# One pair of d_ff chunks by seven block products in tiles 3 to 6, and the visits of scores moved together

## The chip, the cores and the metric

The kernel runs on one core of one Trainium2 chip. The time is the device time of one execution in microseconds. The kernel before took 352.29 us (median of 3 runs, 351.99 to 355.41).

## What is computed

Block-wise causal attention over 8 batches, 8 heads, 576 positions and a head size of 64, and behind it a gated feed-forward network over all 4608 tokens:

```python
scores = scale * np.matmul(q, k.transpose(0, 1, 3, 2))      # q, k, v: 8 x 8 x 576 x 64
scores = np.where(block_i >= block_j, scores, -1e9)         # blocks of 64 positions
attn = np.exp(scores - max); attn = attn / (sum + 1e-09)
x = np.matmul(attn, v)                                      # as 4608 x 512
...
gate = np.maximum(x @ w_gate, 0.0)                          # 512 x 1536
val = x @ w_val                                             # 512 x 1536
return (gate * val @ w_out).astype(np.float32)              # 1536 x 512
```

## The kernel before, in words

The work falls into tiles of 512 tokens, j = 0 to 7 (one for the first 512 positions of each batch), and a ninth one that gathers the last 64 positions of every batch. A tile needs `xT`, the transposed output of its batch's attention. While tile j runs through the feed-forward network, the attention of batch j + 1 is made beside it.

**A tile's two halves.** In the first half d_ff is taken in 12 chunks `f` of 128. For each, four matmuls of 512 columns (the four blocks of d_model) give a gate, which ScalarE (ACT) puts through relu into `gate_sb`, and four give a value; VectorE (DVE) multiplies both into `hT` (`product` L936, `relu` L945, `hidden` L952). Gates and values lie in the three banks `ffnp` of PSUM; each is free again when its relu or its product on DVE has read it. In the second half `hT` times `wo` gives the output. From tile 2 on (`SEVEN`) this is done by seven block products instead of eight (`seven_products` L797), in matmuls of 256 columns; their left sides are sums and differences of chunks of `hT`, made on DVE by `Sums.make_part` (L762). A chunk of `wo` pairs is called c, 0 to 5.

**Pairs.** In tiles 7 and 8 the first half as well takes three pairs of chunks (2 and 3, 4 and 5, 6 and 7; `PAIRS`) by seven block products: `by_pairs` (L963) and in it `pair` (L1019). Their left sides are sums of weights, made once (`up_sum` L713, DVE); their right sides are sums of blocks of x (`x_sums` L905, DVE, into `perm`). The products of a pair accumulate in three places, y, z and m1, which ACT copies and DVE adds in between. In `pair` they are three tiles of their own (`bank` L388, L1023 to L1028).

**A visit of scores.** For each pair of heads (a round r, four a batch) PE writes the scores into two double banks `sc`, into `one` and into an `ffnp` bank; ACT takes their exps in four instructions (two of 512 columns, two of 1024; `visit` L431). The step `s` of a round issues the scores and the first three exps, `e` the fourth exp, `c` zeroes the masked corners on DVE, `a` and `b` multiply by v for the two heads (`head_av` L615, into `one` and `ffnp`) and normalise on DVE, and `x` issues the transposing DMA into `xT` on SP's queue. `L` is the score of the last keys.

**The order.** All engines but the DMAs follow the order in which the program issues (`manual_schedule`). The feed-forward network is a generator that yields after each matmul of 512 columns or two of 256; every other step has a place, a number of yields (`AT` L1325), and runs when the generator has come that far (L1748). A tile has 144 places; `place_of` (L1741) turns places into yields, since tiles from 2 on have 138. In tiles 3 to 6 a round's steps lie 28 places apart, with offsets from `STEADY` (L1608); the loads of q, k (`l`, place 9) and v (`lv`, 46) go on POOL's queue behind a product of `hidden`, and the transposing loads of q and k (`d`, place 66) on SP's. A wait between engines is a semaphore that the layer below the kernel sets from what instructions read and write.

What sets the end of a wait at the change are these lines: the banks of `pair` and the offsets of a round.

```python
y, z, m1 = bank("sc"), bank("one"), bank("sc")                      # pair, L1028
...
STEADY = {"s": 2, "e": 8, "c": 15, "a": 22, "b": 26, "x": 26.1}     # L1608
...
here = ("sc", "sc") if i == 3 else ("one", "ffn")                   # L1707
...
AT[f"{n}{r}"] = base + 28 * i + p                                   # L1710
```

Of the kernel before, what the change touches and what calls it, by code (L numbers as in the profile page):

```python
# [10 lines left out]
FP = mybir.dt.float32  # L11
# [6 lines left out]
def kernel(  # L18
# [20 lines left out]
    FIRST = 3  # L39
    SEVEN = 2  # L40
    PAIRS = (2, 4, 6)
    BASE = {0: 0, 1: 512, 3: 896, 2: 1024}
    AW = 1600
    TW = 256
# [63 lines left out]
    def new_bf():  # L108
        return [sb.tile([128, 2048], BF, name=n, bufs=2) for n in ("q_bf", "k_bf")]
# [603 lines left out]
    def up_sum(n, which):  # L713

        if not ups:
            ups["free"] = [
                t[:, 512 * i : 512 * i + 512].rearrange("p (c f) -> p c f", c=2)  # L720
                for two in (new_bf(), new_bf())
                for t in two
                for i in range(4)
            ]
        i, lo = divmod(PAIRS[n], 4)
        f = slice(128 * lo, 128 * lo + 256)
        g, u = wg[i], wv[i]
        a, b, op = {
            1: (g[:, 0:2, f], u[:, 2:4, f], AX.add),
            2: (u[:, 0:2, f], u[:, 2:4, f], AX.add),  # L730
            5: (g[:, 0:2, f], g[:, 2:4, f], AX.add),
            6: (u[:, 0:2, f], g[:, 0:2, f], AX.subtract),
            7: (g[:, 2:4, f], u[:, 2:4, f], AX.subtract),
        }[which]
        t = ups[n, which] = ups["free"].pop(0)
        nc.vector.tensor_tensor(out=t, in0=a, in1=b, op=op)

    class Sums:
# [58 lines left out]
    def seven_products(j, quads, sums):  # L797

        def times(to, which, p, c, first):
            two = wo[c // 2][:, 2 * (c % 2) : 2 * (c % 2) + 2, :]
            t = sevens[c // 2][:, 768 * (c % 2) : 768 * (c % 2) + 768]
            right = {  # L810
                5: two[:, 1, 256:512],
                2: two[:, 0, 0:256],
                1: t[:, 0:256],
                3: two[:, 0, 256:512],
                4: two[:, 1, 0:256],
                6: t[:, 256:512],
                7: t[:, 512:768],
            }[which]
            nc.tensor.matmul(  # L819
                to,  # L820
                sums.of(c)[which][:, 128 * p : 128 * p + 128],
                right,
                start=first,
                stop=(c == 5),
                skip_group_check=True,
            )

        def half(to, p):
            return to[:, 256 * p : 256 * p + 256]

        early, last = ((0, 1, 2, 3), (4, 5)) if j < B - 1 else ((0, 1, 2, 4), (3, 5))

        def whole(to, which, new=True, cs=range(6)):
            for p in range(2):
                for c in cs:
                    times(half(to, p), which, p, c, new and (p, c) == (0, 0))
                    if c % 2:
                        yield

        def store_later(hi, n0, ob, p0=0, p1=2):  # L840
            if store:
                store.pop()()
            if j < B:
                store.append(lambda: put_block(j, hi, n0, ob, p0, p1))
            else:
                put_block(j, hi, n0, ob, p0, p1)

        y = psum_ffn.tile([128, 512], FP, name="ffnp")
        z = psum_one.tile([128, 512], FP, name="one")
        for to, which in ((y, 5), (z, 2)):  # L850
            yield from whole(to, which, cs=early)
        for to, which in ((y, 5), (z, 2)):
            yield from whole(to, which, new=False, cs=last)
        for q in range(3) if j >= B - 1 else ():
            sums.make_part(q, 1, 0, 2)
        g = sb.tile([128, 512], FP, name="ob", bufs=5)
        nc.scalar.copy(g, y)
        nc.vector.tensor_tensor(out=g, in0=z, in1=g, op=AX.add)
        for q in range(3) if j >= B - 1 else ():
# [12 lines left out]
        yield from whole(z, 4, new=False)  # L872
        c21 = sb.tile([128, 512], FP, name="ob", bufs=5)
        nc.scalar.copy(c21, z)
        store_later(1, 0, c21)
        nc.gpsimd.tensor_tensor(out=g, in0=g, in1=c21, op=AX.add)
        m6 = psum_ffn.tile([128, 512], FP, name="ffnp")
        yield from whole(m6, 6)
        nc.vector.tensor_tensor(out=c22, in0=m6, in1=c22, op=AX.add)
        store_later(1, 256, c22)  # L880
        if j < B:
            m7 = psum_ffn.tile([128, 512], FP, name="ffnp")
            yield from whole(m7, 7)
            nc.vector.tensor_tensor(out=g, in0=g, in1=m7, op=AX.subtract)
            store_later(0, 0, g)
        else:
            for p in range(2):
                m7 = psum_ffn.tile([128, 512], FP, name="ffnp")[:, 0:256]
                for c in range(6):
                    times(m7, 7, p, c, c == 0)  # L890
                    if c % 2:
                        yield
                nc.vector.tensor_tensor(
                    out=half(g, p), in0=half(g, p), in1=m7, op=AX.subtract
                )
                store_later(0, 0, half(g, p), p, p + 1)
# [34 lines left out]
    def ffn_gen():  # L931
        for j in range(B + 1):
# [30 lines left out]
            def by_pairs():  # L963
# [15 lines left out]
                def value(f):  # L979
                    to = psum_ffn.tile([128, 512], FP, name="ffnp")  # L980
                    for c in range(4):
                        product(to, 1, c, f)
                        yield
                    nc.vector.tensor_tensor(
                        out=quads[f // 4][:, f % 4], in0=gates[f], in1=to, op=AX.mult
                    )

                def times(to, n, which, new):
# [30 lines left out]
                def pair(n, first, second, third=()):  # L1019
# [37 lines left out]
                        op1=AX.mult,  # L1057
                    )

                while len(sums.two) < 3:  # L1060
                    sums.two.append(sb.tile([128, 2048], BF, name="stage", bufs=10))
                yield from gate(0)
                store.pop()()
                if j < B:
# [20 lines left out]
                yield from value(11)  # L1085
                sums.make_part(2, 0, 1, 2)

            if j >= B - 1:
                yield from by_pairs()
                yield from seven_products(j, quads, sums)  # L1090
                continue
# [141 lines left out]
    with tc.manual_schedule(engines={E.PE, E.DVE, E.Activation, E.Pool, E.SP}):  # L1233
# [371 lines left out]
            "cv00/23": "pool",  # L1605
            "cv01": "pool",
        }
        STEADY = {"s": 2, "e": 8, "c": 15, "a": 22, "b": 26, "x": 26.1}  # L1608
        acts = {
            "Lq0": lambda: e0.load_qk(0, 2, nc.scalar),  # L1610
            **{f"Lq{h}": lambda h=h: e0.load_qk(h, 2) for h in (2, 4, 6)},
# [91 lines left out]
        for b in range(4, B):  # L1703
            base = 144 * (b - 1)
            for i in range(4):
                r = 4 * b + i
                here = ("sc", "sc") if i == 3 else ("one", "ffn")  # L1707
                acts.update(round_at(r, ("dve", *here, None)))
                for n, p in STEADY.items():
                    AT[f"{n}{r}"] = base + 28 * i + p  # L1710
                    if i == 3 and n in "abx":
                        AT[f"{n}{r}"] += 5
                    if n == "s":
                        AT[f"{n}{r}"] += (0, 1, 2, 1)[i]
            acts[f"L{b}"] = lambda b=b: last_keys(b)
            AT[f"L{b}"] = base + 11
# [10 lines left out]
        acts["X"] = lambda: x_sums(B, (4,))  # L1727
        AT["X"] = 1003
        for i in range(15):
            n, which = i // 5, (5, 2, 1, 6, 7)[i % 5]  # L1730
            acts[f"U{i}"] = lambda n=n, which=which: up_sum(n, which)
            AT[f"U{i}"] = (
                820 + 5 * i if i < 8 else 878 + 28 * (i - 8) if i < 10 else 964 + 8 * (i - 10)
            )
        for c in range(6):
            AT[f"W{c}"] = (225, 229, 233, 242, 266, 270)[c]
# [4 lines left out]
        def place_of(p):  # L1741

            j, o = divmod(p, 144)
            if j < SEVEN:
                return p
            return 144 * SEVEN + 138 * (j - SEVEN) + min(o, 96) + max(0, o - 96) * 42 / 48

        for n in sorted(acts, key=lambda n: AT[n]):  # L1748
            at = int(place_of(AT[n]))
# [33 lines left out]
```

## Time and profile before

| | |
|---|---|
| median of 3 runs | 352.29 us (351.99 to 355.41) |
| the profiled execution's own time | 352.26 us |
| its span, first to last instruction | 350.5 us |
| mean granted TensorE clock | 0.995 |
| tile 4, from its first gate to tile 5's | 213.98 to 251.13 us |
| of it the first half, the second half | 24.32 us, 12.83 us |

PE is TensorE's matmuls, PEld its weight loads, ACT is ScalarE, DVE VectorE, POOL GpSimd, SP the sync engine, which here only issues DMAs. A matmul's row lasts from its start until its result is out; the next one starts much earlier, so the distance of two starts is what a matmul costs on PE. On ACT and DVE too a row's end can overlap the next row's start by about 0.1 us. A row's bracket tells the idle time before it and the instruction that ended it.

### The profile page before, as it was taken

Reading aid. Unit: us, or ns where it says so; the run is one execution under the profiler, and the core shown is the slowest. Engines: PE = TensorE matmul, PEld = TensorE weight load, DVE = VectorE, ACT = ScalarE, POOL = GpSimd, SP = SyncE. Lnnn points to the kernel's source line nnn. Section 1 sums busy time; section 2 is a strip of 40 time slices with the busy share of each in tenths; the row PEclk is TensorE's granted clock in tenths of the full one; section 3 lists DMA queues with packets and bytes.
Section 4 is the critical chain, followed back from the end, with each engine's and each line's share of the span. In section 5 each row is a group of like instructions: output and inputs, shape, how many; then the busy total and the mean of one; then the engine's idle time right before and its main releaser. Section 6 shows DMA issues by size and latency. Waiting matters only on the chain.

```text
span 350.5 us, 8301 instructions
## 1 busy us (share of the span) xinstructions
PE 342.1 (98%) x3245; PEld 208.0 (59%) x3245; DVE 223.9 (64%) x557; ACT 186.0 (53%) x298; POOL 154.9 (44%) x196
## 2 busy tenths in 40 slices
PE   6899999999999999999999999999999999999994
PEld 3554455545545568555855576556755687687673
DVE  4654445768518784467547772668567867986892
ACT  4942757587335862666355546555366525423521
POOL 4857556488966802590149203950300022213213
PEclk9899999999999999999999999999999999999999
DMA  8999989999999996899359944999310031003005
GB/s 245 294 352 373 348 222 280 191 153 177 173 222 107 145 183 129 103 147 165 65 134 138 141 101 124 128 141 143 115 47 15 18 93 51 2 0 123 1 2 120
DMA packets 155399, 50.02 MB, mean 143 GB/s; under 512 B 134464, under 2 KB 151744, under 8 KB 155360
## 3 DMA queue, kind: packets, MB, share of 16 engines
q0 software_dynamic: 70528, 8.98, 48.6%
q1 hardware_dynamic: 76432, 31.47, 43.1%
q10 hardware_dynamic: 8400, 9.05, 8.1%
q8 instruction: 25, 0.41, 0.5%
q14 instruction: 14, 0.11, 0.1%
HBM read 37.75 MB, written 9.44 MB: 135 GB/s over the span
## 4 chain that ended last, share of the span: by engine, by line
PE 94%; DVE 2%; ACT 1%; POOL 1%; issue 0%; POOLq 0%
PE ffnp L937 46%; PE ffnp L819 12%; PE ffnp L1168 6%; PE one L819 5%; PE sc L1003 3%; PE sc L454 3%; PE one L454 2%; PE one L589 2%; PE ffnp L589 2%; PE one L1003 2%; PE one L937 2%; ACT attnT L418 1%; PE sc L589 1%; PE one L1219 1%; PE ffnp L551 1%; PE ffnp L273 1%
## 5 line engine op out<-in xcount | busy, mean ns | idle before, releaser
L947 ACT ACTIVATE gate_sb<-ffnp 128x512 bf16<-128x512 f32 x95 | 57.1, 605 | 74.9 <-PE ffnp L937 70.9
L937 PE MATMUL ffnp<-xT,wg 128*128 128x512 bf16 x356 | 96.7, 379 | 0.0
L937 PE MATMUL ffnp<-xT,wv 128*128 128x512 bf16 x328 | 90.9, 380 | 0.0
L957 DVE TENSOR_TENSOR hT<-gate_sb,ffnp 128x512 bf16<-128x512 bf16 x76 | 52.0, 684 | 45.3 <-PE ffnp L937 28.6
L937 PEld LDWEIGHTS <-wv 128*128 128x128 bf16 x384 | 35.4, 98 | 37.2 <-issue 4.2
L459 ACT ACTIVATE attnT<-sc 128x1024 bf16<-128x1024 f32 x56 | 57.0, 1042 | 0.0
L937 PEld LDWEIGHTS <-wg 128*128 128x128 bf16 x384 | 35.7, 98 | 34.8 <-issue 1.4
L871 POOL TENSOR_TENSOR ob<-ob 128x512 f32<-128x512 f32 x7 | 9.6, 1371 | 102.3 <-ACT ob L868 53.9
L819 PEld LDWEIGHTS <-stage 128*128 128x128 bf16 x420 | 40.3, 98 | 6.0
L778 DVE TENSOR_TENSOR stage<-hT 128x512 bf16<-128x512 bf16 (+2 forms) x82 | 37.8, 493 | 0.9
L589 PEld LDWEIGHTS <-attnT 128*128 128x128 bf16 x640 | 26.7, 98 | 11.7 <-DVE attnT L1228 1.1
L819 PE MATMUL ffnp<-stage 128*128 128x256 bf16 x252 | 31.4, 273 | 0.0
L342 POOL DMA_DIRECT2D q_bf<-in_q_dram x20 | 18.0, 909 | 20.5 <-DVE hT L957 9.7
L466 ACT ACTIVATE attnT<-one 128x512 bf16<-128x512 f32 (+1 forms) x28 | 15.0, 535 | 21.0 <-PE ffnp L454 14.7
L342 POOL DMA_DIRECT2D v_bf<-in_v_dram x30 | 24.2, 878 | 2.4 <-DMA q_bf<-in_q_dram 1.3
L1168 PE MATMUL ffnp<-wo,hT 128*128 128x512 bf16 x96 | 23.6, 379 | 0.0
L454 PEld LDWEIGHTS <-kTm 64*128 64x128 bf16 x384 | 11.0, 94 | 15.1 <-issue 7.9
L342 POOL DMA_DIRECT2D k_bf<-in_k_dram x20 | 18.1, 945 | 0.0
L1034 POOL TENSOR_TENSOR ob<-ob 128x512 f32<-128x512 f32 x6 | 7.7, 1275 | 23.2 <-ACT ob L1033 23.2
L819 PEld LDWEIGHTS <-hT 128*128 128x128 bf16 x168 | 16.4, 98 | 1.9
L454 PE MATMUL sc<-qTm,kTm 64*128 64x512 bf16 (+1 forms) x168 | 16.8, 305 | 0.0
L868 ACT COPY ob<-ffnp 128x512 f32<-128x512 f32 x7 | 4.1, 585 | 22.1 <-PE ffnp L819 22.1
(192 smaller groups left out, 557.1 us busy)
## 6 DMA issues: line engine op xcount, KB each, us to landing
out_dram<-ob ACTq DMA_DIRECT2D x32, 256.0 KB, 2.4
stage<-in_moe_w_val_dram SPq DMA_DIRECT2D x6, 512.0 KB, 8.6
stage<-in_moe_w_gate_dram SPq DMA_DIRECT2D x6, 512.0 KB, 8.6
stage<-in_moe_w_out_dram SPq DMA_DIRECT2D x6, 512.0 KB, 10.6
q_bf<-in_q_dram POOLq DMA_DIRECT2D x20, 128.0 KB, 4.3
k_bf<-in_k_dram POOLq DMA_DIRECT2D x20, 128.0 KB, 5.3
v_bf<-in_v_dram POOLq DMA_DIRECT2D x20, 128.0 KB, 6.2
stage<-in_v_dram SPq DMA_DIRECT2D x19, 128.0 KB, 5.4
```

The lines of the kernel that those rows point to most:

```text
L342: ins = nc.gpsimd.dma_start(dst, part_of)
L454: nc.tensor.matmul(o, kTm[b % 2][head_of(hh), c, hp, :], qT, start=True, stop=True)
L459: return lambda: nc.scalar.activation(at[:, :, lo : lo + 512], sc, AF.Exp, scale=scale)
L466: nc.scalar.activation(at[:, hh, 1024 : 1024 + w], third[hh][:, 0:w], AF.Exp, scale=scale)
L589: nc.tensor.matmul(av[:, p, :], at[:, col : col + 128], v_bf[b % 2][:, c, h, :], start=(p == 0), stop=(c == p), skip_group_check=True,)
L778: nc.vector.tensor_tensor(out=out.rearrange("p (c n) -> p c n", c=m), in0=a, in1=b, op=op)
L819: nc.tensor.matmul(to, sums.of(c)[which][:, 128 * p : 128 * p + 128], right, start=first, stop=(c == 5), skip_group_check=True,)
L937: nc.tensor.matmul(to, (wg, wv)[t][f // 4][:, c, 128 * (f % 4) : 128 * (f % 4) + 128], x[:, c], start=(c == 0), stop=(c == 3),)
L947: nc.scalar.activation(gate_sb, gate, AF.Relu)
L957: nc.vector.tensor_tensor(out=h, in0=gate_sb, in1=val, op=AX.mult)
L1003: nc.tensor.matmul(to[:, 256 * k : 256 * k + 256], left[:, c, 128 * k : 128 * k + 128], right[:, c], start=new and (k, c) == (0, 0), stop= ...
L1168: nc.tensor.matmul(op, hT[f][:, 128 * s : 128 * (s + 1)], wo[f // 4][:, f % 4, n0:n1], start=(f == 0), stop=(f == 11),)
```

## The change

Tiles 3 to 6 (and no longer only 7 and 8) run `by_pairs`, but in a shape of their own. Chunks 0 to 3, 8, 9, 4, 5, 10 and 11 are taken as gate and value, in this order; chunks 6 and 7 are one pair, run by the new function `middle`, behind gate 5. It differs from `pair` in its places: y and z are the two halves of one double bank, m1 is in the other; and z is added to y's copy by DVE, where `pair` copies z too and lets POOL add.

```diff
+                def middle(n, halves):
...
+                    yz = psum_sc.tile([128, 2, 512], FP, name="sc")
+                    y, z = yz[:, 0, :], yz[:, 1, :]
+                    m1 = bank("sc")
+                    low, a, b = ob(), ob(), ob()
+                    yield from times(y, n, 5, True)
+                    nc.scalar.copy(a, y)
+                    yield from times(z, n, 2, True)
+                    nc.vector.tensor_tensor(out=a, in0=z, in1=a, op=AX.add)
+                    yield from halves[0]
+                    yield from times(m1, n, 1, True)
+                    nc.vector.tensor_tensor(out=a, in0=m1, in1=a, op=AX.subtract)
+                    yield from times(y, n, 3, False)
+                    high = relu(y)
+                    yield from times(z, n, 4, False)
+                    nc.scalar.copy(low, z)
+                    yield from halves[1]
+                    yield from times(y, n, 6, False)
+                    nc.vector.tensor_tensor(out=b, in0=y, in1=a, op=AX.add)
+                    yield from times(z, n, 7, False)
+                    nc.vector.tensor_tensor(out=a, in0=z, in1=a, op=AX.add)
+                    nc.vector.tensor_tensor(
+                        out=h[:, :, 256:512], in0=split(high), in1=split(b), op=AX.mult
+                    )
+                    nc.vector.scalar_tensor_tensor(
+                        out=h[:, :, 0:256],
...
+                if j < B - 1:
+                    yield from both(0)
+                    x_sums(j, (1,))
+                    yield from gate(1)
+                    store.pop()()
+                    yield from value(1)
+                    x_sums(j, (3,))
+                    yield from both(2)
+                    x_sums(j, (4, 6))
+                    yield from both(3)
+                    x_sums(j, (7,))
+                    yield from both(8)
+                    sums.make_part(0, 0, 0, 2)
+                    yield from both(9)
+                    sums.make_part(0, 1, 0, 2)
+                    yield from both(4)
+                    sums.make_part(0, 2, 0, 2)
+                    sums.make_part(2, 0, 0, 1)
+                    yield from gate(5)
+                    yield from middle(MIDDLE, (value(5), gate(10)))
+                    yield from value(10)
+                    sums.make_part(1, 0, 0, 2)
+                    yield from gate(11)
+                    yield from value(11)
+                    sums.make_part(2, 0, 1, 2)
+                    return
...
-            if j >= B - 1:
+            if j > SEVEN:
                 yield from by_pairs()
```

In the second half the order of c changes, and parts 1 and 2 of the sums for chunks 4 to 11 are made inside it:

```diff
-        early, last = ((0, 1, 2, 3), (4, 5)) if j < B - 1 else ((0, 1, 2, 4), (3, 5))
+        early, last = ((0, 1, 2, 3), (4, 5)) if j == SEVEN else ((0, 1, 2, 4), (3, 5))
+
+        late_parts = range(3) if j >= B - 1 else (1, 2) if j > SEVEN else ()
```

The four visits of batches 4 to 7 get places of their own, 16 apart and from 5 places before the tile's start, so that the last one's product with v lies in the tile's first half; its banks are `one` and `ffnp` like the others'. The last keys (`L`) go from place 11 to 4. The five weight sums of the pair that tiles 3 to 6 use are made in tile 2's second half, in two buffers `stage` that are kept; those of the other two pairs stay where they were.

```diff
-        STEADY = {"s": 2, "e": 8, "c": 15, "a": 22, "b": 26, "x": 26.1}
+        STEADY = (
+            (-5, 4, 10, 16, 19.5, 19.6),
+            (12, 20, 26, 34, 37.5, 37.6),
+            (28, 36, 42, 50, 53.5, 53.6),
+            (44, 52, 58, 66, 69.5, 69.6),
+        )
...
-                here = ("sc", "sc") if i == 3 else ("one", "ffn")
+                here = ("one", "ffn")
...
-            n, which = i // 5, (5, 2, 1, 6, 7)[i % 5]
+            n, which = (2, 0, 1)[i // 5], (5, 2, 1, 6, 7)[i % 5]
...
-                820 + 5 * i if i < 8 else 878 + 28 * (i - 8) if i < 10 else 964 + 8 * (i - 10)
+                390 + 8 * i if i < 5 else 820 + 8 * (i - 5) if i < 10 else 964 + 8 * (i - 10)
```

More of the change, by code (lines that the diff above doesn't have):

```diff
@@ L41 @@
     PAIRS = (2, 4, 6)
+    MIDDLE = 2
     BASE = {0: 0, 1: 512, 3: 896, 2: 1024}
@@ L713, in up_sum @@
     def up_sum(n, which):
-        if not ups:
-            ups["free"] = [
+        kept = n == MIDDLE
+        if kept not in ups:
+            ups[kept] = [
                 t[:, 512 * i : 512 * i + 512].rearrange("p (c f) -> p c f", c=2)
-                for two in (new_bf(), new_bf())
-                for t in two
+                for t in (
+                    [sb.tile([128, 2048], BF, name="stage", bufs=10) for _ in range(2)]
+                    if kept
+                    else [*new_bf(), *new_bf()]
+                )
                 for i in range(4)
@@ L734, in up_sum @@
         }[which]
-        t = ups[n, which] = ups["free"].pop(0)
+        t = ups[n, which] = ups[kept].pop(0)
         nc.vector.tensor_tensor(out=t, in0=a, in1=b, op=op)
@@ L853, in seven_products @@
             yield from whole(to, which, new=False, cs=last)
-        for q in range(3) if j >= B - 1 else ():
+        for q in late_parts:
             sums.make_part(q, 1, 0, 2)
@@ L858, in seven_products @@
         nc.vector.tensor_tensor(out=g, in0=z, in1=g, op=AX.add)
-        for q in range(3) if j >= B - 1 else ():
+        for q in late_parts:
             sums.make_part(q, 2, 0, 2)
@@ L983, in value @@
                         yield
-                    nc.vector.tensor_tensor(
-                        out=quads[f // 4][:, f % 4], in0=gates[f], in1=to, op=AX.mult
+                    products.append(
+                        nc.vector.tensor_tensor(
+                            out=quads[f // 4][:, f % 4], in0=gates[f], in1=to, op=AX.mult
+                        )
                     )
@@ L1058, in pair @@
                     )
+                def middle(n, halves):
+                    q, k0 = divmod(PAIRS[n], 4)
+                    h = quads[q][:, k0 : k0 + 2]
+                    yz = psum_sc.tile([128, 2, 512], FP, name="sc")
[18 more added lines that the diff above has]
+                    nc.vector.tensor_tensor(out=a, in0=z, in1=a, op=AX.add)
+                    nc.vector.tensor_tensor(
+                        out=h[:, :, 256:512], in0=split(high), in1=split(b), op=AX.mult
+                    )
+                    nc.vector.scalar_tensor_tensor(
+                        out=h[:, :, 0:256],
+                        in0=split(a),
+                        scalar=0.0,
+                        in1=split(low),
+                        op0=AX.max,
+                        op1=AX.mult,
+                    )
@@ L1060, in by_pairs, with both @@
+                def both(f):
+                    yield from gate(f)
+                    yield from value(f)
                 while len(sums.two) < 3:
                     sums.two.append(sb.tile([128, 2048], BF, name="stage", bufs=10))
+                if j < B - 1:
[24 more added lines that the diff above has]
+                    return
@@ L1607 @@
         }
-        STEADY = {"s": 2, "e": 8, "c": 15, "a": 22, "b": 26, "x": 26.1}
+        STEADY = (
[3 more added lines that the diff above has]
+            (44, 52, 58, 66, 69.5, 69.6),
+        )
         acts = {
@@ L1706 @@
                 r = 4 * b + i
-                here = ("sc", "sc") if i == 3 else ("one", "ffn")
+                here = ("one", "ffn")
                 acts.update(round_at(r, ("dve", *here, None)))
[L1709 to L1714, printed above, removed]
+                for n, p in zip("secabx", STEADY[i]):
+                    AT[f"{n}{r}"] = base + p
             acts[f"L{b}"] = lambda b=b: last_keys(b)
-            AT[f"L{b}"] = base + 11
+            AT[f"L{b}"] = base + 4
             if b + 1 < B:
@@ L1745, in place_of @@
                 return p
-            return 144 * SEVEN + 138 * (j - SEVEN) + min(o, 96) + max(0, o - 96) * 42 / 48
+            paired = max(0, j - SEVEN - 1)
+            up = 96 if j == SEVEN else 94
+            return (
+                144 * SEVEN + 138 * (j - SEVEN) - 2 * paired
+                + min(o, up) + max(0, o - 96) * 42 / 48
+            )
         for n in sorted(acts, key=lambda n: AT[n]):
```

## The prediction

> **What bounds the kernel now.** I read the page's list of engines first, then busy time by window for one tile of the steady part (tile 4, 213.98 to 251.13 us), then the timeline around a visit of scores and around a pair by block products, which today only tiles 7 and 8 have.
>
> ```profile
> PE 342.1 (98%) x3245; PEld 208.0 (59%) x3245; DVE 223.9 (64%) x557; ACT 186.0 (53%) x298; POOL 154.9 (44%) x196
> ```
> ```profile
> 213.98:238.30 24.32, 24.32 (x231) 12.28 (x228) 15.42 (x41) 14.93 (x24) 13.76 (x17) 1.00 1.60 129
> 238.30:251.13 12.83, 12.83 (x141) 10.47 (x140) 9.89 (x28) 5.24 (x9) 2.89 (x2) 1.00 0.73 125
> ```
> The window lines give length, then busy time of PE, PEld, DVE, ACT and POOL. In both halves of the tile PE is busy for every microsecond at clock 1.00; the list of PE's waits for 177 to 288 us is empty. So a matmul saved in tiles 3 to 6 is time saved, and any wait put in front of PE is time lost. One visit (222.68 is its first score, 223.44 the matmul behind it):
>
> ```profile
> 222.68 0.28 PE L454 MATMUL one<-qTm,kTm 64*128 64x256 bf16 x1
> ...
> 223.11 0.60 ACT L466 ACTIVATE attnT<-one 128x512 bf16<-128x512 f32 x1 [0.38 <-PE ffnp L454]
> ...
> 223.44 0.39 PE L937 MATMUL ffnp<-xT,wv 128*128 128x512 bf16 x1
> ...
> 223.60 0.59 ACT L466 ACTIVATE attnT<-ffnp 128x512 bf16<-128x512 f32 x1
> 223.67 1.03 PE L937 MATMUL ffnp<-xT,wg 128*128 128x512 bf16 x4
> ...
> 224.08 1.03 ACT L459 ACTIVATE attnT<-sc 128x1024 bf16<-128x1024 f32 x1
> ...
> 224.53 1.03 PE L937 MATMUL ffnp<-xT,wv 128*128 128x512 bf16 x4
> ...
> 224.98 0.62 ACT L947 ACTIVATE gate_sb<-ffnp 128x512 bf16<-128x512 f32 x1
> ...
> 225.66 0.69 DVE L957 TENSOR_TENSOR hT<-gate_sb,ffnp 128x512 bf16<-128x512 bf16 x1 [0.31 <-ACT gate_sb L947]
> ```
> Read from it: four matmuls of 512 columns take 0.86 (223.67 to 224.53), 0.216 each; a relu that stands behind a visit's first three exps starts 2.30 after the first score and ends at 2.92, and its product on DVE ends at 3.67. Now the pair of tile 7:
>
> ```profile
> 291.36 0.60 PE L1003 MATMUL sc<-perm,wg 128*128 128x256 bf16 x4
> 291.79 0.60 PE L1003 MATMUL sc<-perm,wv 128*128 128x256 bf16 x4
> ...
> 291.99 0.60 ACT L947 ACTIVATE gate_sb<-sc 128x512 bf16<-128x512 f32 x1 [1.05 <-PE sc L1003]
> ...
> 293.09 0.60 PE L1003 MATMUL sc<-perm,q_bf 128*128 128x256 bf16 x4
> ...
> 293.53 0.60 PE L1003 MATMUL sc<-perm,k_bf 128*128 128x256 bf16 x4
> 293.79 0.69 DVE L1044 TENSOR_TENSOR ob<-sc,ob 128x512 f32<-128x512 f32 x1 [0.27 <-PE sc L1003]
> ```
> Four matmuls of 256 columns issue in 0.436 (0.109 each) and end 0.60 after the first's start. The product into z (291.79) starts before ACT has read y (291.99), since y and z are two tiles there. ACT follows the last end (291.96) by 0.03, DVE (293.69) by 0.10. And the one place where PE waits for a full bank:
>
> ```profile
> 274.03 0.69 DVE L957 TENSOR_TENSOR hT<-gate_sb,ffnp 128x512 bf16<-128x512 bf16 x1
> ...
> 274.77 0.59 PE L937 MATMUL ffnp<-xT,wv 128*128 128x512 bf16 x2
> ```
> DVE ends at 274.72 and PE goes on 0.05 later: the price of a hand-over to PE.
>
> **The change, part by part.** All in us, for one of tiles 3 to 6.
>
> Columns: chunks 6 and 7 lose 16 matmuls of 0.216 (3.46) and get 28 of 0.109 (3.05): 0.40 less.
>
> Inside the pair: `middle` takes y and z as the two halves of one tile `yz`. In the list of built instructions with their semaphores, z's first matmul of product 2 waits for ACT's copy of y, that of product 4 for ACT's relu of y, and that of product 7 for DVE's sum of y: waits of the tile, not of the data. None of them has other PE work in between.
> Product 2: y's last matmul is issued 0.33 after the pair's start and ends at 0.60; ACT is in gate 5's relu, free at 0.68; the copy takes 0.585 (row below), to 1.26; PE goes on at 1.31 and not at 0.44: 0.88.
> Product 4: relu 0.60 behind 0.60 of matmuls, hand-overs of 0.03 and 0.05: 1.28 against 0.44, lost 0.85 (unrounded).
> Product 7: DVE's sum 0.69, hand-overs 0.10 and 0.05: 1.45 against 0.44, lost 1.01.
> Product 6 also waits, for ACT's copy of z, but gate 10 (0.86) lies in between and the copy ends 0.03 earlier: nothing; if gate 10 were shorter, up to 0.6. Sum 2.74. Bounds: 0 by the rows of tile 7, where z follows y at once; 3.7 if an earlier relu or exp (0.3 of rest each) sits before each reader. I take 2.74, since the listed waits leave no way round.
>
> ```profile
> L1031 ACT COPY ob<-sc 128x512 f32<-128x512 f32 x4 | 2.3, 581 | 0.2 <-PE sc L1003 0.2
> L1051 DVE SCALAR_TENSOR_TENSOR hT<-ob 128x512 bf16<-128x512 f32 x6 | 4.1, 684 | 0.0
> L778 DVE TENSOR_TENSOR stage<-hT 128x1024 bf16<-128x1024 bf16 x8 | 5.1, 683 | 0.0
> ```
>
> The visits: at places 12, 28 and 44 a visit begins just when a gate's four matmuls are issued, so this gate's relu stands on ACT behind the visit's three exps (no visit of tile 4 does that now). By the rows above it ends 2.92 after the first score, and the DVE product that needs it at 3.67.
> Second visit (place 12): scores 0.77, value 1, the first head's product with v (0.45) and three matmuls bring PE to 2.74 at the second head, whose bank is the one that relu 1 must empty: it starts at 2.92 + 0.05, lost 0.24; value 2 then waits for the DVE product behind it, 0.08.
> Third and fourth visit: scores 0.77, a value 0.87, a gate 0.86, the first head 0.45, a matmul of the next value 0.22 and 0.02 of wait for its bank: at 3.19 PE reaches the second head, whose bank a DVE product frees that waits for that same relu: 3.67 + 0.05, lost 0.53 each.
> Sum 1.38. Bounds: 0 by the PE column of the window; 3.1 if each waits one exp longer (three of 1.04). I take the walk, as every step is a row of a visit. The first visit, moved into the output half of the tile before, has its relu 0.5 ahead of need: 0.
>
> The output half: product 10's first matmuls of c 2 need `make_part(1, 0)`, which DVE reaches only after the pair. DVE has the sum (0.69), the product with high (0.68), the one with low (0.69), hidden 10 (0.68) and the part (0.68) to do, each begun 0.08 before the last ends: 3.08. With 0.17 for z's last end and hand-overs of 0.10 and 0.05 that is 3.40 after PE has left the pair; PE spends 2.59 on value 10, gate 11 and value 11 and 0.22 on two matmuls, and waits 0.60. Bounds 0 (today the half starts without a wait) and 1.3 (one more 0.68 ahead of it); I take 0.60.
>
> Moved work that costs nothing: five weight sums (0.41 each on DVE) go from tile 5's output half to tile 2's; five sums of x (0.42 each) and four more ops of 0.69 join DVE, one copy of 0.59 joins ACT, busy 25.3 and 20.2 of 37.1; where either is late it is counted above. SP: the transposes of q and k (4.5 + 4.1 + 1.2 + 1.2 in this trace) now stand behind the third round's transpose, at 20.7 of the tile by my walk instead of 17.7, and end at 32; the last round's two (1.2 each) end at 35; the next first visit is at 39.6. POOL's loads start behind the first hidden product as before. Their cover is the longer tile; in a tile of 36.7 it would be about 2 us, still enough.
>
> Sum per tile: 2.74 + 1.38 + 0.60 - 0.40 = +4.32, a tile of 41.5 instead of 37.15. Four tiles: +17.3. The profiled execution took 352.26 (span 350.5); the median of the runs, 352.29, is the same. Forecast 369.5.
>
> **Where the skill differs.** The Trainium skill, "PSUM — Partial Sum Buffer", section "PSUM bank collisions raise a hardware error", has PSUM guarded by bank and quadrant. y and z lie in different banks, so by that rule the three waits in the pair would not be needed, and the sum by it would be the 358.6 of the third rival below. The built list has them all the same; no row of before has two engines on two banks of one tile, so this trace cannot say more.
>
> **Rivals.**
> Only the pair's waits: the visits and the output half stay covered, as ACT is idle for 46% of a tile and DVE for 32%. 352.3 + 4 x (2.74 - 0.40) = 361.6. Against it: the order on ACT fixes what stands behind what. 0.20.
> More than the walk: waits pass on, each late relu delaying the next visit; above 375. 0.07.
> The pair's waits cost nothing, as between tile 7's y and z; visits and output half as walked: 352.3 + 4 x (1.38 + 0.60 - 0.40) = 358.6. 0.08.
> The other side: the only effect on PE is the columns, since the readers finish in time at every place: 352.3 - 4 x 0.40 = 350.6, no slower. It decides only if all waits of a tile together stay under 0.40, which one copy of 0.585 behind product 5 already exceeds. 0.05.
>
> **How the numbers follow.** The walk has 0.60, the rivals 0.20, 0.07, 0.08 and 0.05. The range of 8 in 10 goes from 361 to 375 and leaves out 358.6, 350.6 and the case above it. A measurement of this kernel tells about 1% from no change: over 1% faster (under 348.8) 0.01, as even the columns alone give 0.5%; within 1% 0.04; over 1% slower (above 355.8) 0.95.
>
> **What would show it.** Right: in each of tiles 3 to 6 three gaps of 0.8 to 1.0 on PE inside the pair, the first two released by ACT, the third by DVE; a gap before the second head's product in the second, third and fourth visit; a gap a few matmuls into the output half; tiles 41 to 42 long. Wrong: PE busy throughout the tile and a period of 36.7; gaps that DMA releases, at the first visit; or a later tile (7, 8) that changes.

## The result and the profile after

The changed kernel takes 369.03 us (median of 6 runs, 368.70 to 369.43) beside 351.93 for the kernel before on the same chip: a ratio of 1.0477 (95% interval 1.0455 to 1.0499; it is worked out from the single runs, so it is not quite the quotient of the two medians). The profiled execution took 368.70, its span is 366.9, its granted clock 0.998. The forecast was 369.5, slower.

The page's list of engines, of the kernel after:

```profile
PE 345.0 (94%) x3293; PEld 211.3 (58%) x3293; DVE 235.6 (64%) x585; ACT 187.8 (51%) x302; POOL 155.1 (42%) x196
```

No engine became the bound: PE stays the busiest, and its share fell from 98% to 94%. A busy time of 345.0 is no measure of the work, since a row lasts until its result is out and rows that no longer overlap add up to more. The page's chain of work that ended last says more; in the kernel before, its share on PE was 94%, on DVE 2% and on ACT 1%:

```profile
PE 70%; ACT 12%; DVE 9%; DMA 3%; issue 2%; POOL 1%; ACTq 1%; SPq 0%; DVEq 0%; POOLq 0%
```

ACT and DVE now stand on the path. Busy time by window for tile 4, first half and second half (length, then PE, PEld, DVE, ACT, POOL, the granted clock, DMA):

```profile
181.43:212.22 30.79, 27.78 (x282) 15.31 (x280) 20.33 (x57) 17.50 (x28) 13.78 (x17) 1.00 1.53 129
212.22:222.82 10.60, 10.26 (x102) 8.47 (x101) 5.58 (x11) 3.20 (x6) 2.53 (x2) 1.00 0.23 68
```

The tile is 41.39 long, where it was 37.15. The clock is 1.00 in both, so nothing here is the clock's. The halves can't be compared one by one with those of before, since a visit moved from one to the other. The list of PE's waits for 170 to 340 us, empty before, has an entry for every place that the prediction named but the second visit (line waited for; us in total, times, longest; it counts three or four tiles, and from a row's modelled end, so that each is shorter than what PE lost, and those of the second visit are too short to be listed):

```profile
PE sc L1012 <- DVE ob L1093: 2.5, 3, 0.8
PE sc L1012 <- ACT ob L1081: 2.2, 3, 0.7
PE ffnp L590 <- DVE hT L992: 2.1, 6, 0.3
PE sc L1012 <- ACT gate_sb L954: 2.1, 3, 0.7
PE ffnp L824 <- DVE stage L783: 1.4, 4, 0.3
```

No DMA is among them. To see what PE lost at each, take the distance between two starts and subtract what the matmuls in between need to issue. The timeline of the kernel after around the pair of tile 4:

```profile
201.19 0.60 PE L1012 MATMUL sc<-xT,stage 128*128 128x256 bf16 x4
...
201.89 0.58 ACT L1081 COPY ob<-sc 128x512 f32<-128x512 f32 x1
...
202.52 0.60 PE L1012 MATMUL sc<-xT,stage 128*128 128x256 bf16 x4 [0.72 <-ACT ob L1081]
...
205.16 0.60 PE L1012 MATMUL sc<-perm,wg 128*128 128x256 bf16 x4
...
205.80 0.60 ACT L954 ACTIVATE gate_sb<-sc 128x512 bf16<-128x512 f32 x1 [3.33 <-PE sc L1012]
...
206.45 0.60 PE L1012 MATMUL sc<-perm,wv 128*128 128x256 bf16 x4 [0.69 <-ACT gate_sb L954]
...
207.76 0.60 PE L1012 MATMUL sc<-perm,stage 128*128 128x256 bf16 x4
...
208.46 0.69 DVE L1093 TENSOR_TENSOR ob<-sc,ob 128x512 f32<-128x512 f32 x1 [1.77 <-PE sc L1012]
...
209.20 0.60 PE L1012 MATMUL sc<-perm,stage 128*128 128x256 bf16 x4 [0.84 <-DVE ob L1093]
```

Four such matmuls issue in 0.44. Product 2 starts 1.33 behind product 5 (202.52 - 201.19), product 4 1.29 behind product 3, product 7 1.44 behind product 6: 0.89, 0.85 and 1.00 lost, 2.74 together. Each time PE goes on within 0.05 of the end of a reader of y, though it writes z. In the trace the first matmul of product 2 and of product 4 itself waits for a semaphore that only ACT's instructions count up, and the first of product 7 for one that only DVE's do.

The second and third visit in the same timeline:

```profile
186.32 0.81 PE L944 MATMUL ffnp<-xT,wg 128*128 128x512 bf16 x3
...
186.54 0.62 ACT L954 ACTIVATE gate_sb<-ffnp 128x512 bf16<-128x512 f32 x1
...
187.21 0.47 PE L590 MATMUL ffnp<-v_bf,attnT 128*128 128x65 bf16 x10
...
187.23 0.67 DVE L992 TENSOR_TENSOR hT<-gate_sb,ffnp 128x512 bf16<-128x512 bf16 x1
...
187.66 0.38 PE L944 MATMUL ffnp<-xT,wg 128*128 128x512 bf16 x1
...
187.95 1.02 PE L944 MATMUL ffnp<-xT,wv 128*128 128x512 bf16 x4
...
192.08 0.62 ACT L954 ACTIVATE gate_sb<-ffnp 128x512 bf16<-128x512 f32 x1
...
192.73 0.69 DVE L992 TENSOR_TENSOR hT<-gate_sb,ffnp 128x512 bf16<-128x512 bf16 x1 [1.92 <-ACT gate_sb L954]
192.75 0.38 PE L944 MATMUL ffnp<-xT,wv 128*128 128x512 bf16 x1
...
193.47 0.46 PE L590 MATMUL ffnp<-v_bf,attnT 128*128 128x65 bf16 x10 [0.35 <-DVE hT L992]
```

Second visit: the second head (L590) starts 0.89 behind three matmuls that issue in 0.65, 0.05 after the relu ends: 0.24; value 2 starts 0.29 behind one of 0.22, as the DVE product ends at 187.90: 0.07. Third visit: 0.72 behind one matmul, 0.05 after a DVE product whose relu was late: 0.50; the fourth repeats it. And the output half:

```profile
212.24 0.68 DVE L783 TENSOR_TENSOR stage<-hT 128x1024 bf16<-128x1024 bf16 x1
212.26 0.38 PE L824 MATMUL ffnp<-wo,stage 128*128 128x256 bf16 x2
...
212.98 0.83 PE L824 MATMUL ffnp<-wo,stage 128*128 128x256 bf16 x6 [0.34 <-DVE stage L783]
```

The third matmul comes 0.72 behind the first, two of 0.11 lie between: 0.50. Per tile 2.74 + 1.32 + 0.50 + 0.03 (the first output matmul behind a relu) - 0.40 = 4.19. From the first gate of tile 2 to that of tile 7 the trace of after has 204.00, that of before 187.02: 16.98, 4.24 a tile. From tile 7's first gate to the end of the last matmul both take 57.6.

### The profile page after: what moved, and what is told of

The parts are those of the page before. It is cut to its first block, busy times and chain, and to the rows that moved or that the text cites. A ratio compares the mean times of both kernels' runs of the same rounds, so it can differ in the third digit from the quotient of the medians.

```text
span 366.9 us, 8410 instructions
## 1 busy us (share of the span) xinstructions
PE 345.0 (94%) x3293; PEld 211.3 (58%) x3293; DVE 235.6 (64%) x585; ACT 187.8 (51%) x302; POOL 155.1 (42%) x196
## 4 chain that ended last, share of the span: by engine, by line
PE 70%; ACT 12%; DVE 9%; DMA 3%; issue 2%; POOL 1%; ACTq 1%; SPq 0%; DVEq 0%; POOLq 0%
PE ffnp L944 27%; PE ffnp L824 10%; PE sc L1012 7%; PE ffnp L1246 6%; ACT attnT L460 5%; PE one L824 5%; ACT gate_sb L954 3%; DVE hT L992 3%; ACT attnT L467 3%; PE ffnp L590 3%; PE one L1012 2%; PE one L944 2%; PE one L590 2%; PE one L455 1%; DMA stage<-in_v_dram 1%
## 5 line engine op out<-in xcount | busy, mean ns | idle before, releaser
L944 PE MATMUL ffnp<-xT,wg 128*128 128x512 bf16 x324 | 87.4, 379 | 0.0
L954 ACT ACTIVATE gate_sb<-ffnp 128x512 bf16<-128x512 f32 x87 | 52.4, 607 | 61.9 <-PE ffnp L944 57.7
L944 PE MATMUL ffnp<-xT,wv 128*128 128x512 bf16 x296 | 81.3, 380 | 0.0
L992 DVE TENSOR_TENSOR hT<-gate_sb,ffnp 128x512 bf16<-128x512 bf16 x52 | 35.3, 679 | 24.3 <-ACT gate_sb L954 20.4
L944 PEld LDWEIGHTS <-wg 128*128 128x128 bf16 x352 | 32.9, 98 | 31.2 <-issue 0.5
L944 PEld LDWEIGHTS <-wv 128*128 128x128 bf16 x352 | 31.3, 98 | 30.1 <-issue 4.6
L824 PEld LDWEIGHTS <-stage 128*128 128x128 bf16 x420 | 40.2, 98 | 9.5 <-DVE stage L783 2.5
L590 PEld LDWEIGHTS <-attnT 128*128 128x128 bf16 x640 | 26.8, 97 | 18.4 <-issue 7.7
L783 DVE TENSOR_TENSOR stage<-hT 128x1024 bf16<-128x1024 bf16 (+2 forms) x74 | 36.6, 528 | 0.5
L824 PE MATMUL ffnp<-stage 128*128 128x256 bf16 x252 | 30.8, 273 | 0.0
L964 DVE TENSOR_TENSOR hT<-gate_sb,ffnp 128x512 bf16<-128x512 bf16 x28 | 19.1, 684 | 15.6 <-PE ffnp L944 13.0
L1012 PEld LDWEIGHTS <-stage 128*128 128x128 bf16 x120 | 11.4, 97 | 12.8 <-issue 7.6
L824 PEld LDWEIGHTS <-hT 128*128 128x128 bf16 x168 | 16.4, 98 | 1.9
```

The costliest lines, as they stand in the source:

```text
L590: nc.tensor.matmul(av[:, p, :], at[:, col : col + 128], v_bf[b % 2][:, c, h, :], start=(p == 0), stop=(c == p), skip_group_check=True,)
L783: nc.vector.tensor_tensor(out=out.rearrange("p (c n) -> p c n", c=m), in0=a, in1=b, op=op)
L824: nc.tensor.matmul(to, sums.of(c)[which][:, 128 * p : 128 * p + 128], right, start=first, stop=(c == 5), skip_group_check=True,)
L944: nc.tensor.matmul(to, (wg, wv)[t][f // 4][:, c, 128 * (f % 4) : 128 * (f % 4) + 128], x[:, c], start=(c == 0), stop=(c == 3),)
L954: nc.scalar.activation(gate_sb, gate, AF.Relu)
L964: nc.vector.tensor_tensor(out=h, in0=gate_sb, in1=val, op=AX.mult)
```

## The experiments

Each is timed beside the kernel before (351.8 to 351.9). Three edits of the changed kernel come first, alone and together, then two other ways to part pair and visits, and then what was left over. Edits are to the changed kernel unless said otherwise.

**Own tiles for y, z and m1.** y and z get a double bank each, m1 an `ffnp` bank.

```diff
-                    yz = psum_sc.tile([128, 2, 512], FP, name="sc")
-                    y, z = yz[:, 0, :], yz[:, 1, :]
-                    m1 = bank("sc")
+                    y, z = bank("sc"), bank("sc")
...
                     yield from halves[0]
+                    m1 = bank("ffn")
```

> Only the places of the pair's three sums change: y and z get a double bank each instead of the halves of one, and m1 a bank of the ring ffnp. My theory (the waits in the pair are those of the shared tile): the three gaps of 0.89, 0.85 and 1.00 us in each of tiles 3 to 6 go, the other gaps stay, and the time falls by 4 x 2.74 = 10.9 to about 358.1 us. Rival (ACT and DVE read y and z too late for the data's own order): the gaps stay or move to the next product that needs the sum, over 366 us.

Measured 360.63, ratio 1.0253 (1.0234 to 1.0272). All three waits are gone, yet the gain is 8.4 and not 4 x 2.74 = 11. PE's waits in this kernel, same window:

```profile
PE ffnp L824 <- DVE stage L783: 2.4, 3, 0.8
PE ffnp L590 <- DVE hT L992: 2.1, 6, 0.3
```

The visits' entry is the same; the output's wait is now 0.8 at its longest, where it was 0.3. PE's loss there rose from 0.50 to 0.95: without the wait ahead of product 7 PE is out of the pair earlier, but the sum behind product 6 and the sum behind product 7 follow each other on DVE. The second one begins 0.65 after PE has left the pair, where it was 0.20. And a wait that had been hidden came out, in the fourth visit:

```profile
200.50 0.31 DVE L1305 MEMSET attnT<- 64x128 uint32 x2
...
200.73 0.35 PE L590 MATMUL one<-v_bf,attnT 128*128 128x65 bf16 x6
```

The first head needs the corners that these two memsets clear, and they stand on DVE behind two parts (1.01). In the changed kernel PE was waiting for the copy of y meanwhile; here it waits 0.20 for them. 0.45 + 0.20 is 0.65 a tile, 2.6 in all, which is the rest.

**Visits one place later.** Places 12, 28 and 44 become 13, 29 and 45, so that the relu of the gate before stands ahead of a visit's exps.

```diff
-            (12, 20, 26, 34, 37.5, 37.6),
-            (28, 36, 42, 50, 53.5, 53.6),
-            (44, 52, 58, 66, 69.5, 69.6),
+            (13, 20, 26, 34, 37.5, 37.6),
+            (29, 36, 42, 50, 53.5, 53.6),
+            (45, 52, 58, 66, 69.5, 69.6),
```

> Only the first step of the second, third and fourth visit moves one place on (13, 29, 45 for 12, 28, 44), so that the gate's relu is issued to ACT ahead of the visit's exps. My theory (the relu behind the exps holds the banks): the gaps of 0.23, 0.08, 0.51 and 0.51 us before the second heads go, 4 x 1.31 = 5.2 us less, about 363.8 us. Rival (four visits within 5.5 us each are too much for ACT, whatever the order): the exps come later instead, the gaps stay or turn up at the first heads, over 367 us.

Measured 364.81, ratio 1.0369 (1.0351 to 1.0386): 4.2 less than the changed kernel, 1.05 a tile. The 0.50 of the third and the fourth visit are gone, so these are the order on ACT, as walked. The second visit's loss stayed, and only moved:

```profile
185.86 0.42 DVE L529 TENSOR_TENSOR xnat<-one,recip 128x256 bf16<-128x256 f32 x1
...
186.20 0.20 DVE L536 TENSOR_TENSOR xtail<-one,recip 64x64 bf16<-64x64 f32 x1
186.33 0.67 DVE L992 TENSOR_TENSOR hT<-gate_sb,ffnp 128x512 bf16<-128x512 bf16 x1
...
186.53 0.38 PE L944 MATMUL ffnp<-xT,wg 128*128 128x512 bf16 x1
...
187.05 1.02 PE L944 MATMUL ffnp<-xT,wv 128*128 128x512 bf16 x4
```

Here relu 1 is long done, and hidden 1 (L992) still starts only at 186.33, behind the first head's normalising (L529, L536). Value 2 starts 0.52 behind one matmul of 0.22: 0.30, about the 0.24 + 0.07 of the changed kernel. So there were two late things at this place, and taking away one showed the other. That is why the gain is 1.0 less than the 5.2 that was expected.

**The output's first part early.** The part that product 10's matmuls wait for is cut in two; chunk 4's share is made before gate 10, inside the pair.

```diff
+                def part_and_gate(f):
+                    sums.make_part(1, 0, 0, 1)
+                    yield from gate(f)
...
-                    yield from middle(MIDDLE, (value(5), gate(10)))
+                    yield from middle(MIDDLE, (value(5), part_and_gate(10)))
                     yield from value(10)
-                    sums.make_part(1, 0, 0, 2)
+                    sums.make_part(1, 0, 1, 2)
```

> Only the sum for chunks 4 and 5 is made apart, ahead of gate 10, and that for chunks 6 and 7 stays behind value 10. My theory (the output half waits for DVE's long chain behind the pair): the gap of 0.51 us at its third matmul goes, 4 x 0.51 = 2.0 us less, about 367.0 us. Rival (DVE is short of time there as a whole): the gap moves to the matmul that needs chunks 6 and 7, no change, 369 us.

Measured 366.68, ratio 1.0418 (1.0403 to 1.0434): 2.35 less, and the entry of L824 is gone from PE's waits.

**All three together.**

> The three edits together. My theory (the three causes are separate and add up): 369.0 - 10.9 - 5.2 - 2.0 = 350.8 us, that is 1.1 us under the kernel before, with tiles of 36.8 us; of the columns' 1.6 us most is kept. Rival (in the shorter tile ACT and DVE, which have more to do than before, are late elsewhere): over 353 us, with new gaps on PE.

Measured 352.69, ratio 1.002 (1.001 to 1.0029). The three edits alone take 8.4 + 4.2 + 2.35 = 15.0, together 16.3: what the first one gave back in the output half is taken by the third, and the corners' 0.20 is gone from the trace too. Left in a tile are the 0.30 ahead of value 2, 0.03 at the first output matmul and 0.10 at a later one; four times this is 1.7 of the 1.9 by which the run lies above what was expected.

**The moved visits without the pair.** Tiles 3 to 6 take chunks 6 and 7 as gate and value again. The sums of weights and of x that the pair would read are still made and not read.

```diff
-                    yield from gate(5)
-                    yield from middle(MIDDLE, (value(5), gate(10)))
-                    yield from value(10)
+                    yield from both(5)
+                    yield from both(6)
+                    yield from both(7)
+                    yield from both(10)
...
-            paired = max(0, j - SEVEN - 1)
-            up = 96 if j == SEVEN else 94
+            paired, up = 0, 96
```

> The moved visits without the pair: tiles 3 to 6 take chunks 6 and 7 as gate and value again (both(5), both(6), both(7), both(10)); the sums that the pair would use are still made and not read. Walk: no pair, so no 2.74, no columns and no output wait from DVE's queue behind the pair; the three visits cost 1.32 a tile as in the changed kernel: 351.8 + 4 x 1.32 = 357.1. Rival (ACT and DVE have room enough without the pair's copies and sums, so the visits cost only where the pair is): 352 to 353.

Measured 358.36, ratio 1.0176 (1.0162 to 1.019): 6.5 more than before, 1.62 a tile and not 1.32. The rival is out: the visits' new places cost this much with no pair near them. Most of the rest is again the clearing of the corners in the fourth visit, 0.21, which the pair's first wait had covered; about 0.1 a tile is not accounted for.

**Work between the products.** `yz` stays one tile, but four matmuls of 512 columns stand between two products that touch it wherever one can be had; the early part is as in the third experiment.

```diff
                     yield from times(y, n, 5, True)
                     nc.scalar.copy(a, y)
+                    yield from halves[0]
                     yield from times(z, n, 2, True)
                     nc.vector.tensor_tensor(out=a, in0=z, in1=a, op=AX.add)
-                    yield from halves[0]
...
                     high = relu(y)
+                    yield from halves[1]
                     yield from times(z, n, 4, False)
                     nc.scalar.copy(low, z)
-                    yield from halves[1]
+                    yield from halves[2]
...
+                    yield from halves[3]
                     yield from times(z, n, 7, False)
...
-                    yield from middle(MIDDLE, (value(5), gate(10)))
-                    yield from value(10)
+                    yield from middle(MIDDLE, (value(5), part_and_gate(10), value(10), gate(11)))
```

> Pair with its one shared tile yz, but with four matmuls of 512 columns (0.86) between two products that touch it: product 5, value 5, product 2, product 1, product 3, gate 10, product 4, value 10, product 6, gate 11, product 7; the output's first part is made before gate 10. If the waits are of the tile, the work between covers all but 0.0 to 0.15 of each (0.85 to 1.01 against 0.86): 368.9 - 4 x (2.7 - 0.3) = 359.3, 358 to 361. If products into the two halves collide in another way (a bank held, not a semaphore), they stay and it is near 366.7.

Measured 365.60, ratio 1.0384 (1.0369 to 1.0398), 6 above what I expected. The waits did shrink where work stands between: product 2's is gone, product 4's too, product 6 has 0.09, product 7 0.23. But value 5 went from in front of product 1 to in front of product 2, and I had not walked product 3, which now has only product 1's 0.44 and a head's 0.45 between it and product 2. The timeline of this kernel:

```profile
201.09 0.58 ACT L1081 COPY ob<-sc 128x512 f32<-128x512 f32 x1
...
202.37 0.60 PE L1012 MATMUL sc<-xT,stage 128*128 128x256 bf16 x4
...
203.27 0.67 DVE L992 TENSOR_TENSOR hT<-gate_sb,ffnp 128x512 bf16<-128x512 bf16 x1
...
203.49 0.38 PE L1012 MATMUL sc<-perm,stage 128*128 128x256 bf16 x2
203.87 0.68 DVE L1084 TENSOR_TENSOR ob<-sc,ob 128x512 f32<-128x512 f32 x1
...
204.59 0.49 PE L1012 MATMUL sc<-perm,wg 128*128 128x256 bf16 x3 [0.73 <-DVE ob L1084]
```

Product 3 (204.59) adds to y, and y's last reader, ACT's copy, ended at 201.67. It starts 0.04 behind the end of L1084, DVE's read of z, which hidden 5 (L992) had delayed: 0.89 lost. The output half waits 0.95, but at another place than in the first experiment: only value 11 now stands between product 7 and the output half, so PE comes to the matmuls of the last chunks before DVE, behind the pair's products and hidden 11, has made their sum (the part ends at 212.84, PE goes on at 212.90). With this, the visits' 1.32 and the corners' 0.21 the tile is 40.5. By its time alone the run would fit the rival (366.7) better than the forecast (359.3); it is the trace that tells them apart: the waits shrink by the work put between, and the one that is left follows whoever last touched the tile, in either half.

**Hidden 1 ahead.** To the kernel with all three edits: the first head that falls into the second visit one place later.

```diff
-            (-5, 4, 10, 16, 19.5, 19.6),
+            (-5, 4, 10, 17, 20.5, 20.6),
```

> The fourth experiment's kernel with the second visit's first head one place later (17, 20.5, 20.6 in place of 16, 19.5, 19.6, in the row of offsets that gives it), so that hidden 1 stands ahead of the first head's normalising on DVE. If the 0.30 ahead of value 2 comes from that order: 352.7 - 4 x 0.30 = 351.5. If hidden 1 is late because its relu is late: unchanged, 352.7.

Measured 351.22, ratio 0.998 (0.9971 to 0.9989): 1.5 less, and the 0.30 is gone from the trace. The order on DVE was the second cause.

**One product on POOL.** To that kernel: the pair's product of high and b on POOL.

```diff
-                    nc.vector.tensor_tensor(
+                    nc.gpsimd.tensor_tensor(
                         out=h[:, :, 256:512], in0=split(high), in1=split(b), op=AX.mult
                     )
```

> The seventh experiment's kernel with one of the pair's two products for hT (high times b) on POOL, which has 1.16 for such a product in the kernel before. DVE's queue behind the pair gets 0.6 shorter, so the last 0.10 in the output half and the 0.11 ahead of it in some tiles go: 351.5 - 4 x 0.15 to 0.2 = 350.8. Rival: POOL's product comes too late for the output's matmuls, or holds up the next loads on its queue: 351.5 or more.

Measured 350.60, ratio 0.9962 (0.9948 to 0.9975): 0.4% below the kernel before, a small gain, but the interval leaves out 1. Tile 4 in this kernel, by window:

```profile
176.95:203.72 26.77, 26.51 (x277) 15.29 (x281) 20.47 (x57) 17.48 (x28) 14.94 (x18) 1.00 1.69 136
203.72:213.76 10.04, 10.04 (x101) 8.54 (x100) 5.51 (x11) 3.18 (x6) 2.53 (x2) 1.00 0.39 99
```

36.81 in all; its list of PE's waits for 170 to 340 us is empty again, and of the gaps only the 0.03 at the first output matmul is left. 37.15 - 36.81 = 0.34 is the columns' 0.40 less that, to 0.03. So this is what the pair is worth once all is covered.

**The pair's waits alone.** To that last kernel: y and z in one tile again.

```diff
-                    y, z = bank("sc"), bank("sc")
+                    yz = psum_sc.tile([128, 2, 512], FP, name="sc")
+                    y, z = yz[:, 0, :], yz[:, 1, :]
+                    m1 = bank("sc")
...
-                    m1 = bank("ffn")
```

> The eighth experiment's kernel with y and z as the two halves of one tile again (and m1 in the other double bank), so that of all the waits of the changed kernel only the pair's three are left. If they cost on PE what their rows say: 350.6 + 4 x 2.74 = 361.6, the time of the rival that only the pair's waits cost anything. Rival (part of the three waits only takes the place of others, as the first experiment gave 2.6 back): here nothing else is left to take the place of, so less than 361 would mean that the waits themselves shrink when the visits stand elsewhere.

Measured 361.52, ratio 1.0287 (1.0253 to 1.0321): 10.9 above the kernel it edits, 2.73 a tile. In its list of PE's waits nothing else is left:

```profile
PE sc L1012 <- DVE ob L1093: 2.5, 3, 0.8
PE sc L1012 <- ACT ob L1081: 2.2, 3, 0.7
PE sc L1012 <- ACT gate_sb L954: 2.1, 3, 0.7
```

## Why the prediction was right, step by step

**The pair's three waits.** Right in place, releaser and size: 0.88, 0.85 and 1.01 walked, 0.89, 0.85 and 1.00 in the trace, and 2.73 by the last experiment, where nothing else is left to mix with. It worked because all that it needs is in rows of the kernel before, of its tiles 6 and 7: the reader's duration, two hand-overs, and the time in which four matmuls issue. Product 6, walked at nothing, lost nothing.

**What the three waits are.** The rival that they cost nothing is out. The Trainium skill, "PSUM — Partial Sum Buffer", section "PSUM bank collisions raise a hardware error", has PSUM guarded by bank and quadrant, and no run here goes against that: with a tile each, a product into z runs beside the copy of y (0.58 there too) and waits for nothing. The waits belong to the tile that both halves share: by the first and the last experiment they go and come with it (m1 changes its bank too, but none of the three waits is in front of a product into m1), and in the sixth a product into y waits for the read of z. With a tile each, y and z also lie in two different double banks, so the times alone would allow that the two banks of one double bank get in each other's way; against this stand the semaphores on which the three matmuls wait in the trace.

**The visits.** 1.38 walked, 1.32 measured (0.24, 0.07, and 0.50 twice, before rounding). For the third and fourth the cause is the one walked, since one place later they are gone. For the second I named the relu, which was only one of two late things: the product on DVE stood behind the first head's normalising as well, and cost the same 0.30 once the relu was early. That did not touch the forecast, but an edit built on it would have gained nothing there.

**The output half.** 0.60 walked, 0.50 measured. The five operations on DVE took 3.09 (209.83 to 212.92) where 3.08 was walked, but they began 0.20 after PE had left the pair (209.83 - 209.63) and not 0.27: here DVE followed product 7's last end by 0.03, where the row of tile 7 had 0.10. Another 0.03 went to the first output matmul, whose bank a relu emptied late; that was not walked.

**The columns.** 0.40 walked; 0.34 net of the 0.03 wait, measured where all else is covered.

**Covers.** None of the waits is a DMA's, and tiles 7 and 8 are unchanged, as forecast. SP's transposes of q and k ended 28.6 into the tile and the last round's 31.8, where I had walked 32 and 35; the next first visit came at 39.5.

**The sum.** 4.32 a tile, 4.24 measured; 17.3 in all, and 17.1 between the two medians (369.03 and 351.93). No term is off by more than 0.1, so the sum does not rest on errors that cancel. Adding the terms was safe only because I took all of them at once. Taken one by one they do not add: two waits (the corners' 0.20 and 0.45 of the output's) lie hidden under the pair's, so whoever removed only the pair's would have got three quarters of it.

**The rival on the other side** (only the columns count, 350.6) is what the kernel gives when nothing waits: 350.60 in the eighth experiment. It failed for the reason given beside it: one copy behind product 5 costs more than all that the columns save. That the two times agree so closely is partly luck: the rival takes 1.6 off 352.3, the experiment lies 1.28 below its own 351.88. In the same way the rival of the pair's waits alone, 361.6, is met by 361.52 in a kernel in which the other waits had been removed, but that is 9.7 above the kernel before and not 9.4; in the changed kernel the other waits were there.

## What to carry to other kernels

A buffer that is split in two was here still one buffer to whatever sets the waits; two accumulators that are read in turn need a tile each, or work for PE in between, or PE pays for the reader at every change between them. When a stage is full on one engine, a change that saves 0.40 there is decided by the waits that it adds anywhere, so walk each reader's place on its engine before counting columns. After taking a wait away, look for what had been hidden under it: here a quarter of the gain went to one wait that grew and one that no trace had shown before.

## What was not expected of the hardware

A DVE operation slowed down beside one on POOL. With the pair's product on POOL, the operation on DVE that follows (128x512 from two operands in SBUF) took 0.93 in all four tiles, and 0.68 in the kernel that differs from it in this alone:

```profile
L1098 DVE SCALAR_TENSOR_TENSOR hT<-ob x4: 928/932/936, 165.7 to 276.1; 128x512 bf16<-128x512 f32 x4
```

The two rows of tile 4 in this kernel's timeline:

```profile
201.71 1.16 POOL L1095 TENSOR_TENSOR hT<-gate_sb,ob 128x512 bf16<-128x512 bf16 x1 [7.69 <-DVE ob L1092]
...
202.49 0.94 DVE L1098 SCALAR_TENSOR_TENSOR hT<-ob 128x512 bf16<-128x512 f32 x1
```

They overlap by 0.38 (POOL's product lasts from 201.71 to 202.87, DVE's operation starts at 202.49), and the operation is 0.25 longer. The sum ahead of it (L1094, one operand in PSUM), which POOL's product overlaps whole, kept its 0.69. So the move took 0.68 off DVE's queue and gave 0.25 back. The Trainium skill, "SBUF — State Buffer", section "Who interferes with whom", says that a DVE instruction with two SBUF inputs contends with a GpSimd instruction that reads SBUF, and one with at most one, outside the two-port modes, does not; the two rows agree on who is hit. It calls the port an exclusive lock; a block for the whole overlap would give 0.68 + 0.38 = 1.06, an estimate from these rows; the trace has 0.93, and as spans on POOL are rough this run can't tell a full block from a partial one.
